# A recurrent memory branch on one core: five weight buffers in flight instead of four, 21 streamed slices instead of 20, in a new order

## The chip, the cores and the metric

One core of one Trainium2 chip. The metric is the device time of one execution in microseconds, as a median of several. Ratios are computed as the mean time of one kernel's runs over the mean of the kernel before in the same rounds on the same chip. They are therefore not quite the ratios of the medians quoted beside them, and they are what to compare across sessions: the median of the kernel before itself was 2405 to 2430 us from session to session.

## The reference

The result is `g * a + (1 - g) * b`. `a` is sliding window attention over 2048 tokens of width 640. `b` is an attention with a memory, and it takes most of the time:

```python
for s in range(n_seg):                       # 64 segments of 32 tokens
    h = concat([mem, x[s]])                  # 8 memory rows + 32 tokens
    q, k, v = h @ Wq, h @ Wk, h @ Wv         # 640 -> 32 heads x 192, three times
    p = softmax(where(mask, q @ k.T * scale, -1e9))
    o = (p @ v) @ Wo                         # 32 x 192 -> 640
    mem, out[s] = o[:8], o[8:]               # the next segment needs these 8 rows
```

The segments are a chain. The four weights have 7.9 MB each in bf16, and only part of them stays in the core's memory (SBUF) in both kernels.

## The kernel before

Heads are worked in four groups. The weights are cut into 84 slices: per group five each of q, k and v (128 x 1536, 384 KB) and six of o (128 x 1280, 320 KB). Of these, 64 are loaded once and stay. The other 20 are streamed again from HBM in each segment, through a ring of buffers. A slice "lands" when its transfer is complete. A buffer is "released" by the last matmul that reads it, and only then can the transfer of a later slice into it be issued. The projections of the last eight tokens of each segment do not depend on the chain. They are made for all segments before it, with a ring of their own, and are called the tails below:

```python
sb = {"w": (4, [P, WQ]), ...}                # the ring of weight buffers
STREAMED = {"q": ((), (4,), (4,), (3, 4)), "k": ((4,), (4,), (4,), (4,)), "v": ((), (), (4,), ()),
            "o": ((1, 3, 5), (1, 3, 5), (2, 5), (1, 3, 5))}

def load_w(u):
    ...
    if u not in weights.slot:
        return None                          # resident
    b = sc.buf("w")
    sc.op("SP", 100 + 0.78 * weights.width(u), lambda: nc.sync.dma_start(
        tile_of(b)[:, 0:weights.width(u)], weights.dram_of(u)), writes=[b])
    return b
```

A list fixes the order of TensorE in a segment. `q0` is the query projection of group 0 (five slices, streamed ones last), `tq0` its transposes, `s0` the scores, `p0` the transposed probabilities, `pv0` the values, `o0` the output projection (six slices):

```python
STEP = "q0 k0 tq0 tk0 k1 q1 s0 tk1 tq1 v0 k2 q2 s1 tk2 k3 p0 tq2 q3 s2 pv0 v1 p1 o0 tq3 pv1 tk3 v2 p2 s3 o1 pv2 v3 p3 o2 pv3 o3"
```

A small list scheduler with assumed durations orders the other engines and the DMA queue while the kernel is built; the chip sees only the order.

## Time and profile before

| | before |
|---|---|
| median of 3 runs | 2416.04 us (2411.96 to 2423.39) |
| memory branch | 560 to 2371 us of the span of 2406 |
| one segment, mean | 28.3 us |
| streamed per segment | 20 slices, 7.14 MB |
| TensorE busy, share of the span | 88% |

The first fence is the page's row of issues for the ring: how often, how large, and the median from issue to landing. The second is the page's DMA share and rate in 40 slices of the span.

```profile
t_w<-w_packed SPq DMA_DIRECT2D x704, 320.0 KB, 4.1
t_w<-w_packed SPq DMA_DIRECT2D x584, 384.0 KB, 4.4
```

```profile
DMA  4222224777888887888888888878888887888887
GB/s 138 69 66 62 65 73 131 239 227 232 266 265 271 274 276 255 273 272 267 270 263 288 272 272 283 268 253 264 256 272 273 280 263 248 268 278 275 264 277 232
```

1280 of these 1288 transfers belong to the 64 segments; the long even stretch at 248 to 288 GB/s is the memory branch. The prediction shows the rest.

### The profile page before, as it was taken

Reading aid. Unit: us, or ns where it says so; the run is one execution under the profiler, and the core shown is the slowest. Engines: PE = TensorE matmul, PEld = TensorE weight load, DVE = VectorE, ACT = ScalarE, POOL = GpSimd, SP = SyncE. Lnnn points to the kernel's source line nnn. Section 1 sums busy time; section 2 is a strip of 40 time slices with the busy share of each in tenths; the row PEclk is TensorE's granted clock in tenths of the full one; section 3 lists DMA queues with packets and bytes.
Section 4 is the critical chain, followed back from the end, with each engine's and each line's share of the span. In section 5 each row is a group of like instructions: output and inputs, shape, how many; then the busy total and the mean of one; then the engine's idle time right before and its main releaser. Section 6 shows DMA issues by size and latency. Waiting matters only on the chain.

```text
span 2406.0 us, 112716 instructions
## 1 busy us (share of the span) xinstructions
PE 2122.8 (88%) x49058; PEld 1523.4 (63%) x49093; DVE 1131.1 (47%) x3942; ACT 1045.4 (43%) x2385; POOL 741.7 (31%) x2055
## 2 busy tenths in 40 slices
PE   7999998998888888988889899888888888888885
PEld 5777767975666665666666666655666665666663
DVE  6888882233444433444444444444343443444334
ACT  4888883223333333433333344333333433333333
POOL 5555552123222222222222222222222222222220
PEclk9999988999999999999999999999999998999997
DMA  4222224777888887888888888878888887888887
GB/s 138 69 66 62 65 73 131 239 227 232 266 265 271 274 276 255 273 272 267 270 263 288 272 272 283 268 253 264 256 272 273 280 263 248 268 278 275 264 277 232
DMA packets 256880, 561.55 MB, mean 233 GB/s; under 512 B 54648, under 2 KB 70272, under 8 KB 256384
## 3 DMA queue, kind: packets, MB, share of 16 engines
q1 hardware_dynamic: 230608, 507.05, 64.9%
q0 software_dynamic: 21504, 43.03, 6.0%
q8 instruction: 385, 6.31, 1.0%
q10 hardware_dynamic: 4272, 4.26, 0.6%
q14 instruction: 111, 0.91, 0.1%
HBM read 524.83 MB, written 36.51 MB: 233 GB/s over the span
## 4 chain that ended last, share of the span: by engine, by line
PE 59%; DMA 35%; ACT 3%; issue 1%; DVE 1%; POOL 0%; SPq 0%; ACTq 0%; DVEq 0%; POOLq 0%
DMA t_w<-w_packed 33%; PE ps_o L946 8%; PE ps_k L776 8%; PE ps_q L776 8%; PE ps_v L776 6%; PE p_m L282 4%; PE p_s L327 3%; PE t_psum L590 3%; PE ps_pv L922 3%; PE tr_k L791 2%; PE t_psum L610 2%; PE p_o L411 2%; PE S_ps L848 2%; PE tr_q L791 1%; PE p_st L327 1%
## 5 line engine op out<-in xcount | busy, mean ns | idle before, releaser
L776 PEld LDWEIGHTS <-t_hT 128*32 128x32 bf16 x15360 | 380.2, 98 | 291.7 <-issue 65.7
L946 PE MATMUL ps_o<-t_OT,t_w 128*128 128x40 bf16 x7040 | 290.1, 180 | 104.9 <-DMA t_w<-w_packed 99.0
L946 PE MATMUL ps_o<-t_OT,w_o 128*128 128x40 bf16 x8320 | 321.4, 180 | 47.2 <-ACT t_OT L927 45.2
L946 PEld LDWEIGHTS <-t_w 128*128 128x128 bf16 x7040 | 226.5, 96 | 127.7 <-DMA t_w<-w_packed 125.5
L946 PEld LDWEIGHTS <-w_o 128*128 128x128 bf16 x8320 | 267.7, 96 | 55.4 <-issue 45.9
L823 POOL COPY t_K<-t_xqk 128x64 bf16<-128x64 bf16 x256 | 60.9, 238 | 776.2 <-PE S_ps L848 776.2
L357 DVE CUSTOM_DVE_ANT_0 a_junk<-p_s,a_mask 128x384 bf16<-128x384 f32 (+2 forms) x512 | 253.5, 529 | 41.4 <-PE p_st L327 29.0
L776 PE MATMUL ps_v<-w_v,t_hT 128*32 128x384 bf16 x4864 | 252.4, 336 | 0.0
L927 ACT CAST t_OT<-ps_pv 128x480 bf16<-128x480 f32 x256 | 143.2, 559 | 248.2 <-PE ps_pv L922 244.6
L776 PE MATMUL ps_q<-w_q,t_hT 128*32 128x384 bf16 x4096 | 222.0, 339 | 18.7 <-DVE t_hT L957 18.4
L387 ACT ACTIVATE a_pt<-p_st 128x384 bf16<-128x384 f32 (+2 forms) x512 | 219.8, 474 | 42.6 <-PE p_st L327 34.6
L814 DVE COPY t_K<-tr_k 128x256 bf16<-128x256 bf16 x256 | 74.7, 292 | 333.7 <-PE tr_k L791 333.4
L776 PE MATMUL ps_k<-w_k,t_hT 128*32 128x384 bf16 x4096 | 219.9, 336 | 0.1
L781 ACT CAST t_tok<-ps_k 128x384 bf16<-128x384 f32 x256 | 122.7, 479 | 207.5 <-PE ps_k L776 201.8
L800 ACT COPY b_QT<-tr_q 128x384 bf16<-128x384 bf16 x256 | 123.3, 481 | 175.7 <-PE tr_q L791 175.7
L905 DVE TENSOR_TENSOR t_PTx<-PT_ps,mk_x 128x320 bf16<-128x320 f32 x256 | 126.0, 492 | 143.1 <-PE PT_ps L898 143.1
L395 POOL TENSOR_SCALAR_AFFINE_SELECT a_pt<-a_pt 128x512 bf16<-128x512 bf16 x240 | 148.1, 640 | 128.9 <-ACT a_pt L387 128.2
L781 ACT CAST t_tok<-ps_q 128x384 bf16<-128x384 f32 x256 | 122.6, 479 | 149.5 <-PE ps_q L776 140.7
L858 DVE TENSOR_REDUCE sm_mx<-S_ps 128x4 f32<-128x160 f32 x256 | 82.4, 322 | 209.7 <-PE S_ps L848 208.1
L781 ACT CAST t_vtok<-ps_v 128x384 bf16<-128x384 f32 x256 | 122.7, 479 | 102.2 <-PE ps_v L776 102.2
L734 POOL DMA_DIRECT2D t_xqk<-xbqk x256 | 137.9, 539 | 80.1 <-POOL b_QT L804 40.0
L327 PE MATMUL p_st<-a_qa,a_k 64*128 64x128 bf16 x1440 | 148.2, 223 | 5.2 <-ACT a_pt L387 3.5
(144 smaller groups left out, 4052.3 us busy)
## 6 DMA issues: line engine op xcount, KB each, us to landing
t_w<-w_packed SPq DMA_DIRECT2D x704, 320.0 KB, 4.1
t_w<-w_packed SPq DMA_DIRECT2D x584, 384.0 KB, 4.4
t_xqk<-xbqk POOLq DMA_DIRECT2D x256, 48.0 KB, 3.6
xbqk<-t_ts POOLq DMA_DIRECT2D x12, 768.0 KB, 5.9
w_v<-in_B_Wv_dram SPq DMA_DIRECT2D x19, 384.0 KB, 8.2
w_q<-in_B_Wq_dram SPq DMA_DIRECT2D x16, 384.0 KB, 5.7
w_k<-in_B_Wk_dram SPq DMA_DIRECT2D x16, 384.0 KB, 4.2
xbv<-t_ts POOLq DMA_DIRECT2D x16, 384.0 KB, 3.7
```

Source lines behind the costliest of these rows:

```text
L282: nc.tensor.matmul(view()[:, gg, :], lhsT=Wp[:, kt, 4 * g:4 * g + 4, :].rearrange("p h d -> p (h d)"), rhs=T(k["xT"])[:, kt, :], start=(kt ...
L327: nc.tensor.matmul(T(out)[:, i * P:(i + 1) * P], lhsT=b if keys_first else a, rhs=a if keys_first else b, start=True, stop=True, tile_posi ...
L357: sc.op("DVE", 135 + n / 0.96, lambda: nc.vector.tensor_tensor_reduce(out=T(junk)[:, 0:n], in0=T(s)[:, 0:n], in1=mask[:, NKB * P - n:], op ...
L387: sc.op("ACT", act_ns(n), lambda: nc.scalar.activation(out=T(pt)[:, h % 4, 0:n], in_=T(s)[:, 0:n], func=ACT.Exp), reads=[s], writes=[pt])
L395: nc.gpsimd.affine_select(out=v, in_=v, compare_op=op, fill=0.0, base=0, pattern=[[0, 4], [sign, P]], channel_multiplier=-sign)
L734: sc.op("DMA", 500, lambda: nc.gpsimd.dma_start(tile_of(qk)[:].rearrange("p i b t -> p (i b t)"), xbqk[s, :, g].rearrange("p i c -> p (i c ...
L776: nc.tensor.matmul(t[32 * j:32 * j + 32, 0:384], lhsT=tile_of(hT)[:, kt, :], rhs=w[:, j * 384:(j + 1) * 384], start=(kt == kts[0]), stop=( ...
L781: sc.op("ACT", act(384), lambda: nc.scalar.copy(tile_of(tok)[:], b["tile"][:, 0:384]), reads=[b], writes=[tok])
L800: nc.scalar.copy(dst, tq["tile"][:].rearrange("p b (j t) -> p b j t", t=SEG))
L905: nc.vector.tensor_tensor(out=tile_of(dst)[:], in0=PT["tile"][:, i, :, :].unsqueeze(2).to_broadcast([P, 2, 4, L]), in1=mk.unsqueeze(1).uns ...
L927: sc.op("ACT", act(480), lambda: nc.scalar.copy(tile_of(OT)[:].rearrange("p b j l -> p (b j l)"), o["tile"][:, 0:480]), reads=[o], writes= ...
L946: nc.tensor.matmul(t[:, dt * L:(dt + 1) * L], lhsT=w[:, r * D + dt * P:r * D + (dt + 1) * P], rhs=OT["tile"][:, b, i, :], start=(g == 0 an ...
```

## The change

Its intent: let each transfer start one buffer earlier, pay for the buffer's 3072 bytes per partition by streaming one slice more, and spread the streamed slices so that they are needed at even distances.

```diff
-    LAT = {..., "SP": 2000}
+    LAT = {..., "SP": 3200}
-STEP = "q0 k0 tq0 tk0 k1 q1 s0 tk1 tq1 v0 k2 q2 s1 tk2 k3 p0 tq2 q3 s2 pv0 v1 p1 o0 tq3 pv1 tk3 v2 p2 s3 o1 pv2 v3 p3 o2 pv3 o3"
+STEP = "q0 k0 v0 tk0 tq0 k1 q1 s0 tk1 tq1 q2 s1 tq2 k2 k3 p0 tk2 q3 pv0 v1 s2 p1 o0 tk3 tq3 pv1 v2 s3 p2 o1 pv2 v3 p3 o2 pv3 o3"
-        "w": (4, [P, WQ]), ...
+        "w": (5, [P, WQ]), ...
-        sc.op("SP", 100 + 0.78 * weights.width(u), ...
+        sc.op("SP", 60 + 0.755 * weights.width(u), ...
-STREAMED = {"q": ((), (4,), (4,), (3, 4)), "k": ((4,), (4,), (4,), (4,)), "v": ((), (), (4,), ()),
-            "o": ((1, 3, 5), (1, 3, 5), (2, 5), (1, 3, 5))}
+STREAMED = {"q": ((), (), (3, 4), (4,)), "k": ((4,), (3, 4), (4,), (4,)), "v": ((), (4,), (4,), (4,)),
+            "o": ((1, 3, 5), (2, 5), (2, 5), (1, 3, 5))}
```

More of the change, by code (lines that the diff above doesn't have):

```diff
@@ L19 @@
 class Sched:
-    LAT = {"PE": 190, "DVE": 125, "ACT": 140, "POOL": 150, "DMA": 2000, "SP": 2000}
+    LAT = {"PE": 190, "DVE": 125, "ACT": 140, "POOL": 150, "DMA": 2000, "SP": 3200}
     SWITCH = 100
@@ L651, in branch_B @@
     sb = {
-        "w": (4, [P, WQ]), "hT": (1, [P, KT, SEG]), "tok": (2, [P, 384]), "vtok": (1, [P, 384]), "K02": (1, [P, 4, 2, L]),
+        "w": (5, [P, WQ]), "hT": (1, [P, KT, SEG]), "tok": (2, [P, 384]), "vtok": (1, [P, 384]), "K02": (1, [P, 4, 2, L]),
         "PTm": (1, [P, 2, 4, L]), "PTx": (1, [P, 2, 4, L]), "OT": (1, [P, 3, 4, L]), "Pm": (1, [P, 4, SEG]),
@@ L743, in load_w @@
         b = sc.buf("w")
-        sc.op("SP", 100 + 0.78 * weights.width(u), lambda: nc.sync.dma_start(tile_of(b)[:, 0:weights.width(u)], weights.dram_of(u)),
+        sc.op("SP", 60 + 0.755 * weights.width(u), lambda: nc.sync.dma_start(tile_of(b)[:, 0:weights.width(u)], weights.dram_of(u)),
               writes=[b])
```

## The prediction

> **What bounds the kernel now.** I read the page's slices first, then the windows of the long stage, then the chain, then the waits of TensorE and of the DMA queue, and last single slices in the timeline.
>
> The 40 slices show three stages: attention and tails to about 560 us, then one uniform stage to about 2371 us, then a short mix. The uniform stage is the memory branch: 64 segments one after another, since each needs the memory rows that the one before made. Three windows of it:
>
> ```profile
> 700.00:1200.00 500.00, 440.28 (x11133) 307.30 (x11129) 210.05 (x726) 192.81 (x443) 136.82 (x425) 0.98 0.83 269
> 1200.00:1700.00 500.00, 438.48 (x11164) 308.00 (x11168) 207.89 (x716) 191.75 (x440) 136.28 (x421) 0.99 0.83 269
> 1700.00:2200.00 500.00, 442.24 (x11198) 309.98 (x11187) 211.61 (x732) 192.79 (x443) 137.34 (x426) 0.97 0.83 269
> ```
>
> TensorE (first pair) is busy 88%, its clock is nearly full (0.97 to 0.99), the vector engines are under half busy, the DMA engines have 0.83 and move 269 GB/s. Nothing is full: two nearly full resources wait for each other. The chain says which:
>
> ```profile
> PE 59%; DMA 35%; ACT 3%; issue 1%; DVE 1%; POOL 0%; SPq 0%; ACTq 0%; DVEq 0%; POOLq 0%
> DMA t_w<-w_packed 33%; PE ps_o L946 8%; PE ps_k L776 8%; PE ps_q L776 8%; PE ps_v L776 6%; PE p_m L282 4%; PE p_s L327 3%; PE t_psum L590 3%; PE ps_pv L922 3%; PE tr_k L791 2%; PE t_psum L610 2%; PE p_o L411 2%; PE S_ps L848 2%; PE tr_q L791 1%; PE p_st L327 1%
> ```
>
> Weight slices streamed into the ring t_w carry 33% of the chain. That is not 33% to win: while a transfer is on the chain, TensorE works on other things. What is to win is TensorE's idle time, from its waits between 700 and 2300 us:
>
> ```profile
> PE ps_o L946 <- DMA t_w<-w_packed: 84.9, 133, 1.9
> PE ps_o L946 <- ACT t_OT L927: 39.6, 56, 0.7
> PE ps_q L776 <- DVE t_hT L957: 16.6, 57, 0.3
> PE tr_k L791 <- ACT t_tok L781: 16.5, 54, 0.3
> PE ps_q L776 <- DMA t_w<-w_packed: 13.8, 29, 1.6
> PE ps_k L776 <- DMA t_w<-w_packed: 6.3, 14, 0.8
> PE ps_v L776 <- DMA t_w<-w_packed: 2.0, 4, 0.7
> ```
>
> The four DMA rows make 107 us, but undercount, as the timeline shows:
>
> ```profile
> 1424.30 0.40 PE L946 MATMUL ps_o<-t_OT,t_w 128*128 128x40 bf16 x10
> 1424.55 0.40 PE L946 MATMUL ps_o<-t_OT,w_o 128*128 128x40 bf16 x10
> 1425.20 0.42 PE L946 MATMUL ps_o<-t_OT,t_w 128*128 128x40 bf16 x10 [0.25 <-DMA t_w<-w_packed]
> 1425.47 0.41 PE L946 MATMUL ps_o<-t_OT,w_o 128*128 128x40 bf16 x10
> ```
>
> Groups of ten start 0.25 us apart but count as busy for 0.40. A start 0.65 after the last has lost 0.40 us, and only 0.25 is called idle; a delay below 0.15 is not seen. So I took starts: for each streamed slice, the distance from the start of the matmul before it, less the usual spacing (0.025 us for output slices, 0.152 for projection slices). Over segments 5 to 61 this gives 2.85 us lost per segment, of a mean segment of 28.33 us. The worst positions are the third slice of the first output group (0.72), the last of the fourth (0.49) and the second of the fourth query chunk (0.33).
>
> The queue's own side, same window:
>
> ```profile
> SPq L744 <- PE ps_o L946: 367.7, 400, 3.4
> SPq L744 <- DMA t_w<-w_packed: 236.8, 374, 2.3
> DMA to landing us min/median/max: 2.9/4.2/7.7
> ```
>
> The issuing queue mostly stands waiting for TensorE to free a buffer. The loop is: buffer freed, issue, about 4.3 us to landing, wait for its turn, use.
>
> [...] its best 20 us window (440 to 460, other loads) has 313 GB/s at share 0.95. [...] a slice issued with one other slice in flight lands after 3.96 us, with two after 4.33, with three after 4.53.
>
> **The change, part by part.**
>
> *Fifth buffer.* Each transfer follows the release of the slice five places before it instead of four. In the trace the gap between those two releases is 0.5 to 2.7 us depending on place, 1.4 on average (28.33/20). All mean losses above are below that, so with unchanged transfers nearly all 2.85 us would go.
>
> *One slice more.* Before: q 4, k 4, v 1, o 11 = 20 slices, 9 x 393 KB + 11 x 328 KB = 7.14 MB per segment. After: q 3, k 5, v 3, o 10 = 21 slices, 7.60 MB (+6.4%). Smaller streams, estimated as 269 GB/s x 28.33 us - 7.14 MB, add 0.48 MB. So 8.08 MB must flow per segment.
>
> *Order.* The chunk v0 moves in front of the first transposes. That fills the wait of tr_k for t_tok: 16.5 us over 57 segments, 0.29 us each. The price: between the first and the second score group only q2 is left (before: v0, k2, q2). From score start to the next score I count 0.44 (scores) + 0.27 + 0.27 (transposes) + 0.82 (q2); the vector work for the new K then has about 1.4 us after the first scores for some 1.2 us (0.32 + 0.29 + 0.30 + 0.27). It fits narrowly; I allow 0 to 0.1. The waits for t_hT (0.29) and for t_OT before the last output group (0.7) stay.
>
> *Choice.* Streamed v slices now stand between the output groups, and the first half of a segment uses 9 slices instead of 8. Demand is more even.
>
> *Scheduler constants.* They emit nothing; the order of TensorE is fixed by the list, that of the queue stays by need.
>
> *Tails stage.* Its ring remains at three. The second group now needs three streamed slices, and its second must wait for the first group's last product, where before the third group had a wait of 1.2 us. About one more landing shows: +3 us once.
>
> Sum: without any waits for slices a segment takes 28.33 - 2.85 - 0.29 = 25.2 us. A buffer's turn is then 5 x 25.2 / 21 = 6.0 us (before: 4 x 28.33 / 20 = 5.67, made of 4.33 landing, 0.90 waiting for its turn, 0.2 use, 0.3 from release to reissue). With about 3.8 in flight instead of 3.1 (21 x 4.7 / 26.5 against 20 x 4.33 / 28.33), I set landing at 4.7 us. That leaves 6.0 - 4.7 - 0.5 = 0.8 us of slack, not more than the 0.9 of now, if nothing were lost. So losses do not vanish; they fall until turn and slack agree. Before: mean lateness 2.85/20 = 0.143, mean wait 0.90, as of a spread with mean 0.76 and deviation 1.04 us. The same spread with the new balance (mean = 0.80 + 4 x lateness) gives 0.077 us per slice, 21 x 0.077 = 1.6 us. Segment: 25.2 + 1.6 = 26.8. Gain 1.53 us x 64 = 98, less 3 in the tails: 2416 - 95 = 2321 us, 3.9% less.
>
> **Rivals.**
>
> *The transfers become the bound.* 8.08 MB at 330 GB/s (313/0.95) need 24.5 us per segment; at 26.8 us they flow at 301 GB/s, share about 0.92. If landing grows to 5.2 us under that load, the fifth buffer only holds a slower transfer, and the added 6.4% eat the rest: segments of 27.6 to 28, time 2375 to 2400. For it: share 0.83 already, landing grows with depth. Against: 0.95 was sustained for 20 us, and growth from two to three others was only 0.2 us. I give it 0.15.
>
> *All losses go.* With evener demand the spread shrinks, and the segment nears 25.4 to 25.8: 2255 to 2285. For it: every mean loss is below the gain from one more buffer. Against: the slack above. 0.12.
>
> *A compute wait takes over.* K or Q of the second scores late by 0.3 us and more: +20 us, so 2340. Possible on top of either.
>
> *Clock.* A busier TensorE might be granted less; 0.98 to 0.96 would cost some 0.3 us per segment, 20 us. The tails show 1.00 at 100% busy, which speaks against it.
>
> **Range and chances.** 2321 us; 2280 to 2372 holds it 8 times in 10, from near the all-go case to a mild form of the bandwidth rival. The 2% line is 2368. Faster by over 2%: 0.83; within 2%: 0.15; slower by over 2%: 0.02, as only saturation with longer landing would do it.
>
> **What would show it.** Right: segments near 26.8 us, GB/s near 300 and share 0.91 to 0.93 in the three windows; landing median 4.5 to 4.9 us; the four DMA rows of TensorE's waits down to roughly half of 107 us; the row tr_k for t_tok gone; no new row above 10 us at the second scores; the tails some 3 us longer. Wrong: landing above 5.2 with GB/s at 290 or less (bandwidth), new waits of S_ps for K or QT, a clock under 0.95, or DMA waits of TensorE as large as before.

## The result, and the profile after

| | before | after |
|---|---|---|
| median of 4 runs each | 2419.72 us (2411.96 to 2435.53) | 2290.39 us (2278.75 to 2298.31) |
| ratio | | 0.9454 (95%: 0.9386 to 0.9522) |
| segment, between output stores | 28.30 us | 26.20 us |
| lost to slices per segment | 2.86 us | 0.90 us |

Segments are measured here between the stores of two segments' outputs (segments 5 to 60), so that runs without slices can be measured alike. The loss is counted from the starts of matmuls as the prediction does. The time is 5.5% less; 3.9% was predicted.

The same three windows of the long stage (the columns are those of the prediction's first fence; the last two are DMA share and GB/s):

```profile
700.00:1200.00 500.00, 456.27 (x12060) 327.62 (x12056) 218.73 (x779) 209.83 (x475) 146.60 (x456) 0.99 0.93 307
1200.00:1700.00 500.00, 460.13 (x12156) 329.96 (x12151) 220.22 (x782) 212.50 (x481) 148.26 (x459) 1.00 0.93 311
1700.00:2200.00 500.00, 460.56 (x11986) 328.86 (x11985) 218.70 (x777) 209.00 (x473) 146.59 (x456) 0.98 0.92 306
```

TensorE is busy for about 459 of 500 us instead of 440, and the transfers follow: 308 GB/s instead of 269. On the chain of work that ended last, the transfers have 23% instead of 35%, and TensorE 68% instead of 59%:

```profile
PE 68%; DMA 23%; ACT 4%; issue 3%; DVE 1%; POOL 1%; SPq 0%; ACTq 0%; POOLq 0%; DVEq 0%
```

TensorE's waits, over 1600 us again (600 to 2200 us; us in total, times, longest):

```profile
PE ps_o L946 <- ACT t_OT L927: 43.1, 61, 0.7
PE ps_q L776 <- DVE t_hT L957: 20.4, 61, 1.7
PE ps_o L946 <- issue: 13.8, 20, 1.6
PE tr_q L791 <- ACT t_tok L781: 12.3, 59, 0.2
PE ps_o L946 <- DMA t_w<-w_packed: 12.2, 41, 1.0
PE ps_k L776 <- DMA t_w<-w_packed: 8.6, 17, 1.4
PE ps_v L776 <- issue: 7.8, 8, 2.6
PE ps_v L776 <- DMA t_w<-w_packed: 4.6, 8, 1.8
```

The rows for slices (DMA t_w) make 26 us with a last one of 0.6 that is not shown, against 107 before. The wait of tr_k for t_tok has gone, but a smaller one of tr_q has come in its place. And there are rows that end in "issue", 26 us in all with four small ones not shown: TensorE stood idle and no wait that the profile shows explains it. Before, one such row had 1.9 us. The queue and its landings, same window:

```profile
SPq L744 <- PE ps_o L946: 287.9, 407, 2.8
DMA to landing us min/median/max: 3.2/4.8/7.9
```

### The profile page after: what moved, and what is told of

Its sections match the earlier page's. It is cut to its first block, busy times and chain, and to the rows that moved or that the text cites.

```text
span 2283.2 us, 112848 instructions
## 1 busy us (share of the span) xinstructions
PE 2070.3 (91%) x49058; PEld 1508.2 (66%) x49093; DVE 1109.1 (49%) x3942; ACT 1054.5 (46%) x2385; POOL 737.9 (32%) x2055
## 3 DMA queue, kind: packets, MB, share of 16 engines
q8 instruction: 384, 6.29, 1.1%
## 4 chain that ended last, share of the span: by engine, by line
PE 68%; DMA 23%; ACT 4%; issue 3%; DVE 1%; POOL 1%; SPq 0%; ACTq 0%; POOLq 0%; DVEq 0%
DMA t_w<-w_packed 19%; PE ps_o L946 12%; PE ps_k L776 9%; PE ps_q L776 8%; PE ps_v L776 7%; PE ps_pv L922 4%; PE p_m L282 4%; PE p_s L327 4%; PE t_psum L590 3%; PE tr_q L791 2%; PE tr_k L791 2%; PE t_psum L610 2%; PE p_o L411 2%; PE S_ps L848 1%; PE p_st L327 1%
## 5 line engine op out<-in xcount | busy, mean ns | idle before, releaser
L776 PEld LDWEIGHTS <-t_hT 128*32 128x32 bf16 x15360 | 372.6, 97 | 281.5 <-issue 54.8
L946 PE MATMUL ps_o<-t_OT,w_o 128*128 128x40 bf16 x8960 | 329.7, 180 | 58.0 <-ACT t_OT L927 45.2
L946 PEld LDWEIGHTS <-w_o 128*128 128x128 bf16 x8960 | 281.7, 96 | 66.8 <-issue 57.3
L946 PE MATMUL ps_o<-t_OT,t_w 128*128 128x40 bf16 x6400 | 264.1, 180 | 21.5 <-DMA t_w<-w_packed 14.5
L357 DVE CUSTOM_DVE_ANT_0 a_junk<-p_s,a_mask 128x384 bf16<-128x384 f32 (+2 forms) x512 | 253.3, 528 | 40.7 <-PE p_st L327 29.4
L776 PE MATMUL ps_q<-w_q,t_hT 128*32 128x384 bf16 x4352 | 230.9, 336 | 22.1 <-DVE t_hT L957 21.0
L776 PE MATMUL ps_v<-w_v,t_hT 128*32 128x384 bf16 x4352 | 228.1, 330 | 6.6 <-issue 6.5
L946 PEld LDWEIGHTS <-t_w 128*128 128x128 bf16 x6400 | 207.3, 96 | 32.9 <-DMA t_w<-w_packed 25.8
L776 PE MATMUL ps_k<-w_k,t_hT 128*32 128x384 bf16 x3840 | 206.0, 332 | 0.3 <-issue 0.2
```

The source lines that it names most:

```text
L357: sc.op("DVE", 135 + n / 0.96, lambda: nc.vector.tensor_tensor_reduce(out=T(junk)[:, 0:n], in0=T(s)[:, 0:n], in1=mask[:, NKB * P - n:], op ...
L776: nc.tensor.matmul(t[32 * j:32 * j + 32, 0:384], lhsT=tile_of(hT)[:, kt, :], rhs=w[:, j * 384:(j + 1) * 384], start=(kt == kts[0]), stop=( ...
L946: nc.tensor.matmul(t[:, dt * L:(dt + 1) * L], lhsT=w[:, r * D + dt * P:r * D + (dt + 1) * P], rhs=OT["tile"][:, b, i, :], start=(g == 0 an ...
```

## The experiments

Twelve kernels. All of them passed the comparison with the reference, even the three that compute with wrong weights, so that comparison says little about this branch; the other nine do the kernel's own arithmetic. "Segment" and "loss" are as in the table above.

| run | buffers | slices | ratio to before (95%) | segment us | loss us |
|---|---|---|---|---|---|
| before | 4 | 20 | 1 | 28.30 | 2.86 |
| order_alone | 4 | 20 | 0.9972 (0.9905 to 1.0039) | 28.14 | 3.09 |
| four_buffers | 4 | 21 | 1.0155 (1.0125 to 1.0184) | 29.05 | 3.64 |
| old_order_old_choice | 5 | 21 | 0.9757 (0.9705 to 0.9809) | 27.64 | 1.94 |
| new_order_old_choice | 5 | 21 | 0.9666 (0.9633 to 0.9699) | 27.14 | 1.83 |
| old_order_new_choice | 5 | 21 | 0.9657 (0.9619 to 0.9695) | 27.01 | 1.12 |
| after | 5 | 21 | 0.9454 (0.9386 to 0.9522) | 26.20 | 0.90 |
| old_constants | 5 | 21 | 0.9540 (0.9492 to 0.9587) | 26.36 | 1.19 |
| split_output | 5 | 21 | 0.9571 (0.9512 to 0.9630) | 26.83 | 1.81 |
| six_buffers | 6 | 22 | 0.9420 (0.9370 to 0.9469) | 26.05 | 0.36 |
| six_buffers_split | 6 | 22 | 0.9505 (0.9463 to 0.9547) | 26.70 | 1.50 |
| no_slices_before | | 0 | 0.9114 (0.9075 to 0.9154) | 24.99 | 0 |
| no_slices_after | | 0 | 0.8996 (0.8956 to 0.9036) | 24.46 | 0 |

### four_buffers: is it the buffer?

```diff
-        "w": (5, [P, WQ]), ...
+        "w": (4, [P, WQ]), ...
```

(in the kernel after)

> The changed kernel with its order, its choice of 21 slices and its constants, but four buffers in the ring again. Theory A (the fifth buffer carries the gain, because a buffer's turn 4 x T / 21 leaves hardly any slack over a landing of 4.5 us): segments of about 28.8 us, some 2440 us in all, slightly slower than the kernel before, with over 3 us per segment lost to slices. Theory B (the new order and choice carry most of the gain, the buffer is secondary): 2355 us or less, segments under 27.4 us.

Measured: 2463.54 us against 2423.76, 1.6% slower than before, segments of 29.05 us and 3.64 us of loss. Theory A was close (28.8 us and over 3, though the whole time is 23 us above its 2440), theory B is out. Its windows show a machine with room to spare that does not use it:

```profile
700.00:1200.00 500.00, 435.02 (x10930) 307.31 (x10926) 198.01 (x700) 189.58 (x429) 133.29 (x412) 0.96 0.87 280
1200.00:1700.00 500.00, 435.68 (x10802) 304.20 (x10798) 198.12 (x699) 189.14 (x428) 131.14 (x408) 0.95 0.85 276
```

The new order and choice, without the fifth buffer, are a loss: one slice more in a ring that already turned too slowly. The clock (0.95 to 0.96, against 0.97 to 0.99 before) is lower as well, to which the last section returns.

### order_alone: the order in the kernel before

The edit is the line STEP of the diff alone, in the kernel before.

> The kernel before with the new order alone: four buffers, the old 20 slices. If the order is worth the wait of tr_k for t_tok and that wait is on the path: 18 us less, about 2400. If time won there is waited for at the next slice (ring of four sets the pace): 2416 plus or minus 10, and loss to slices rises above 2.85 us per segment.

Measured: 2397.62 against 2405.58 us, ratio 0.9972, which is unclear from no change. The loss rose from 2.86 to 3.09 us. Without slices the same order is worth 0.53 us per segment (below); here the segment is only 0.16 us shorter, and 0.23 us have come back as waits at slices. That is what the second reading said of the loss. The time itself does not decide: 2397.62 us is near the first reading's 2400, but the kernel before was faster in the same rounds too (2405.58), and 18 us less (a ratio of 0.993) lies within the interval.

### Order and choice, each alone, with five buffers

For the old choice, the old 20 slices cannot be kept, as the fifth buffer then finds no room (the build refuses it: a pool asks for 0.94 KB per partition and 0.56 are left). One slice of v was added:

```diff
-STREAMED = {"q": ((), (), (3, 4), (4,)), "k": ((4,), (3, 4), (4,), (4,)), "v": ((), (4,), (4,), (4,)),
-            "o": ((1, 3, 5), (2, 5), (2, 5), (1, 3, 5))}
+STREAMED = {"q": ((), (4,), (4,), (3, 4)), "k": ((4,), (4,), (4,), (4,)), "v": ((), (4,), (4,), ()),
+            "o": ((1, 3, 5), (1, 3, 5), (2, 5), (1, 3, 5))}
```

The old order is the old line STEP. Both edits together, then each alone:

> Five buffers and 21 slices, but the old order and the old choice (the old 20 slices plus one of v). Theory A' (evener demand from the new order and choice shrank the lateness below what I predicted; with the old ones the predicted size holds): segments of 27.1 us (26.8 plus the 0.29 of the wait for t_tok), 2338 us, loss near 1.6 us per segment. Theory B' (the fifth buffer shrinks lateness by itself, my estimate was simply too careful): 2308 us, segments near 26.65, loss near 0.9.

> Five buffers and the new order, with the old choice plus one slice of v (10 projection and 11 output slices, 7.54 MB against 7.60). If the choice of slices evens the demand: about 2315 to 2325 us and loss of 1.2 us or more per segment, most of it at the output groups. If the choice does not matter: within 0.5% of the changed kernel, 2290.

> Five buffers and the new choice with the old order. If the order is worth only the wait of tr_k for t_tok: 0.29 us x 64 = 18 us over the changed kernel, 2308 us. If the order also evens the demand for slices: 2320 us or more, loss per segment above 1.2 us.

Measured: 2367.28, 2344.12 and 2344.25 us, beside 2423.76 for the kernel before. Five buffers with the old order and choice give only 2.4% of the 5.5%. Their loss of 1.94 us is near, and a little above, the 1.6 that I had predicted for the change itself. So theory A' is the nearer one: what I had left out is what the new order and choice do to the evenness of the demand. The first two were 29 and 19 us slower than even the higher of my numbers. The third falls under the "2320 us or more" of its second reading, but its loss of 1.12 us is not above the 1.2 that went with it.

The loss tells the two apart. The choice lowers it from 1.94 to 1.12 in the old order and from 1.83 to 0.90 in the new. The order lowers it by 0.1 to 0.2 and otherwise shortens the segment itself. In time, with five buffers, the order alone is worth 0.9% and the choice alone 1.0%, but both together 3.0% (0.9757 against 0.9454, measured at different times). Whether they really help each other, or the two measurements differ by themselves, is not shown.

Why the old choice loses is seen in one place. This is the timeline of old_order_old_choice at the end of its first output group (start, duration, and in brackets the idle time before):

```profile
1404.23 0.41 PE L946 MATMUL ps_o<-t_OT,t_w 128*128 128x40 bf16 x10
1404.48 0.41 PE L946 MATMUL ps_o<-t_OT,w_o 128*128 128x40 bf16 x10
1406.19 0.42 PE L946 MATMUL ps_o<-t_OT,t_w 128*128 128x40 bf16 x10 [1.30 <-DMA t_w<-w_packed]
```

The third streamed slice of `o0` is late in each of the 57 segments counted, by 1.33 us on average: two thirds of all loss. Its transfer follows the release of the slice five places earlier, the first of the two of `q3`. On average that one is released 9.3 us after the use of the segment's first streamed slice begins, and the transfer is issued at 9.5. TensorE would be ready for it at 12.8 (14.1 less the loss of 1.33). So it has 3.3 us for a landing of 4.6. In the new choice `q3` has one slice, and the one five places earlier is that of `k3`. With the order unchanged (old_order_new_choice) the transfer is then issued 0.8 us earlier and needed 0.5 us later, so that it has 4.6 us, and the loss at this place is 0.17. In the kernel after it is 0.22. The rule of this ring is therefore not a mean: for each slice, TensorE's work between the release five places back and the use has to exceed a landing and the reissue (4.6 and 0.2 us at this place).

### no_slices: the segment without any wait for slices

```diff
     def load_w(u):
         ...
-        if u not in weights.slot:
-            return None
+        return None
     def w_of(u, b):
-        return weights.tiles[u] if b is None else b["tile"]
+        return weights.tiles.get(u) or weights.tiles[("o", 0, 0) if u[0] == "o" else ("v", 0, 0)]
```

The result is wrong, the instructions of TensorE are the same in number and shape. The edit was made in the kernel before and in the one after. (The 26.36 us of the second expectation is the mean over all segments of the kernel after.)

> The kernel before with no slice streamed in the memory branch; a resident slice stands in for each (wrong result on purpose). This measures a segment without waits for slices in the old order. From the starts of the matmuls I had 28.33 - 2.85 = 25.48 us per segment, so 2416 - 182 = 2234 us. If my count of lost time was too high (part of it clock or other waits), it stays above 2260; if delays hide behind others, it goes below 2215.

> The same in the changed kernel's order. By the step of the prediction (the new order takes away 0.29 us) a segment is 25.2 us: 18 us under the run with the old order. By the changed kernel's trace (26.36 - 0.91 = 25.45 us) the new order gains nothing without slices: within 5 us of the run with the old order, near 2232 us.

Measured: 2195.32 and 2166.02 us beside 2405.58. Both are lower than I expected. Segments are 24.99 and 24.46 us. So the kernel before lost 28.30 - 24.99 = 3.31 us per segment to streaming, with whatever traffic and clock cost besides the waits, and not only the 2.85 that I had counted. And the order is worth 0.53 us by itself, not 0.29: the inference from the trace of after that it gains nothing was wrong. The waits for t_tok account for little of it (17.5 us in 56 segments as against 13.1 in 61, so 0.1 us). The rest lies between the matmuls: the distances from the last start of one output tile to the first of another sum to 7.23 us per segment in the old order and to 6.52 in the new, where other kinds of work stand next to each other. Which of these pairs matter most was not separated. I had counted waits only.

### old_constants

```diff
-    LAT = {..., "SP": 3200}      and 60 + 0.755 * weights.width(u)
+    LAT = {..., "SP": 2000}      and 100 + 0.78 * weights.width(u)
```

> The changed kernel with the scheduler's two old cost constants. In the memory branch the build differs by one pair of vector instructions, in the tails by the order of the queue. Within 0.5% of the changed kernel (2279 to 2302 us). A rival by which the constants matter would show over 1%.

Measured: 2297.87 us, ratio 0.9540 where the kernel after has 0.9454, from another session, and the intervals touch. The median lies in the band that I had given. The two ratios differ by 0.9%, with an uncertainty as large, so an effect on the whole time is not shown, and one of 1% is not excluded either.

One effect does show, in the tails. The branch's first streamed slice is used at 560.0 us here, as in the kernel before (560.3), and at 564.1 in the kernel after. TensorE's wait of 3.0 us there, for `t_ts` at L610, stands in the trace of after and, with 3.0 and 2.4 us, in the two runs with the old choice and the new constants. Here, in the kernel before and in order_alone it is 0.3 us at most. So the constants lengthen the tails, and the choice of slices does not.

### six_buffers: would one more still help?

```diff
-        "w": (5, [P, WQ]), ...
+        "w": (6, [P, WQ]), ...
-"v": ((), (4,), (4,), (4,)),
+"v": ((4,), (4,), (4,), (4,)),
```

> The changed kernel with a sixth buffer, paid for by a 22nd slice (one of v0): 8.47 MB per segment with the small streams. If buffers still decide: loss falls under 0.4 us, 2255 us or so. If bandwidth now decides (at the share of 0.93 and 310 GB/s seen with five, 8.47 MB need 27.3 us): 2320 to 2350 us with landing above 5.5 us and GB/s no higher than 320.

Measured: 2282.81 us beside 2426.60, ratio 0.9420. The time lies between the two expectations and is not told apart from the kernel after (0.9454; the intervals overlap). The loss to slices fell to 0.36 us as the first reading said, and 325 GB/s were reached, more than the second allowed:

```profile
700.00:1200.00 500.00, 455.14 (x12150) 327.68 (x12151) 218.81 (x782) 211.40 (x478) 149.01 (x459) 0.99 0.95 325
```

Yet TensorE got no more work done. Its waits, 600 to 2200 us, say what came in the place of the slices:

```profile
PE ps_o L946 <- issue: 25.0, 35, 1.8
PE ps_v L776 <- issue: 11.9, 9, 2.2
PE ps_k L776 <- DMA t_w<-w_packed: 9.2, 16, 2.8
```

The rows "issue" make 51 us in all here, twice those of the kernel after.

### split_output: a wait that was not worth removing

The last output group waits 0.7 us for t_OT in each segment. A second buffer for t_OT fits (with one set of softmax statistics instead of three), and the output groups can be cut so that other output work stands in the gap:

```diff
-... s3 p2 o1 pv2 v3 p3 o2 pv3 o3
+... s3 p2 oa1 pv2 v3 p3 ob1 oa2 pv3 ob2 o3      # o1 cut after 5 slices, o2 after 4
-"OT": (1, ...)    b_stats bufs=3
+"OT": (2, ...)    b_stats bufs=1
```

> The changed kernel with a second buffer for t_OT and the second and third output groups cut, so that two pieces of output work stand between the last values and the last output group, which now waits 0.7 us for t_OT. If that wait is on the path and transfers can follow: 0.5 us x 64 = 32 us less, about 2258 us. If the transfers, at share 0.93, now set the pace: less than 12 us, 2278 to 2290, with the loss to slices up by 0.3 us per segment or more.

Measured: 2322.73 us beside 2426.60, ratio 0.9571: slower than the kernel after, and slower than even my second reading, though by the loss that it named. The wait for t_OT is gone, and this has come (600 to 2200 us, lines shifted by one):

```profile
PE ps_o L947 <- DMA t_w<-w_packed: 53.4, 109, 1.9
PE ps_q L777 <- DVE t_hT L958: 17.2, 59, 0.3
PE ps_o L947 <- issue: 14.8, 23, 1.4
```

The three streamed slices of the last output group lose 0.10, 0.44 and 0.56 us; in the kernel after they lost 0.08 together. They are needed 0.7 us earlier now (their waits taken off), but their transfers are not issued earlier. The second one is even issued 1.3 us later (18.9 us after the segment's first streamed slice instead of 17.6), since the slice of `v3` now stands five places before it. It is the same rule as above: the gap for t_OT had been time in which slices landed. Bandwidth does not explain it, since the rate fell to 299 to 303 GB/s. The smaller number of statistics buffers was not tested alone; TensorE has no wait for scores above 0.7 us in this trace.

### unread_slices: the transfers alone

```diff
     def load_w(u):
         ...
-        return b
+        return None
```

and the stand-in of the run without slices: all 21 slices are transferred into the ring, and no matmul reads them.

> The changed kernel's 21 slices per segment are all transferred into the ring of five, but no matmul reads them (a resident slice stands in, wrong result on purpose), so that nothing waits for them and the queue runs as fast as five in flight allow. It shows what the transfers alone can do, and whether their mere traffic costs TensorE time. If the stalls that the profile calls issue come from instruction fetches delayed by traffic: such stalls appear in TensorE's waits although no slice is waited for (they were absent without slices), and the time is 10 to 40 us over the run without slices (2166). If they belong to the coupling with slices: 2166 plus or minus 8 and no such stall. Transfers alone: if bandwidth bounds the changed kernel, no more than 320 GB/s in the memory branch; if its pace came from buffers coming free, 335 GB/s or more.

The whole time, 2645.25 us, answers nothing. I had overlooked that two resident output slices are loaded by the same queue: they stood behind the unread stream, and TensorE waited for them once for 376 us. What remains is useful, since the stream ran ahead and ended at about 1980 us. One program therefore has a stretch with traffic and one without, and TensorE waits for no slice in either:

```profile
1100.00:1800.00 700.00, 625.40 (x16036) 443.20 (x16036) 284.52 (x1030) 281.78 (x633) 195.01 (x604) 0.95 0.99 350
2050.00:2600.00 550.00, 522.10 (x14234) 379.90 (x14234) 253.93 (x921) 248.68 (x559) 173.53 (x538) 1.00 0.08 19
```

Transfers through five buffers move 350 GB/s when nothing holds them, and 363 to 381 in each 100 us from 600 to 900 us, while TensorE stood idle. So the 308 of the kernel after is not the limit of the transfers: its pace came from buffers coming free. That was the expectation of 335 or more. And segments take 27.56 us in the first stretch (26 of them) and 24.47 in the second (23). Mere traffic costs 3.1 us per segment here. The waits of the first stretch:

```profile
PE ps_q L776 <- DVE t_hT L957: 18.8, 26, 2.2
PE ps_o L946 <- issue: 18.8, 19, 1.5
PE ps_pv L922 <- issue: 3.7, 3, 2.2
```

In the second there is no row "issue". Stalls of this kind over 0.25 us sum to 29.4 us in 26 segments, 1.1 us each; the wait for t_hT is 0.7 us each instead of 0.3 (the small load of x, t_hT<-xa_dram, lands after 4.7 us at the median of this run, 3.6 in the kernel before); and the clock is 0.95 instead of 1.00, by estimate from these two at most 5% of a segment or 1.4 us. Together that is at most 2.9 of the 3.1.

What are the stalls? The trace has the packets of the queue that the page calls instruction (q8: 384 packets and 6.29 MB in the kernel after, so 16 KB each). In the kernel after, 29 stalls over 0.25 us between 700 and 2200 us ended 1.41 us after the landing of such a packet at the median, nine in ten within 1.56; in six_buffers 54 stalls, 1.40 and 1.55; in this run 45 stalls, 1.43 and 1.55. A random moment is 2.6 to 3.3 us after the last one at the median. So the stalls end some 1.4 us after such a packet lands. From this timing and the name of the queue I take it that TensorE stood waiting for its next instructions; no run moved these packets, so this is not shown. The packets themselves hardly slowed (0.98 us before, 1.01 to 1.05 in these, and 1.05 in no_slices_after, which has no stall), so slower packets do not explain the stalls; whether they started late was not measured.

### six_buffers_split

The edits of the last two variants together, five rounds.

> Six buffers with 22 slices and the cut output groups. Six buffers left 0.36 us of loss per segment, and cutting takes away up to 0.5 us of wait for t_OT. If the cut failed because a ring of five cannot follow the crowded output slices: with six it gains, 2255 to 2270 us. If at share 0.95 bandwidth takes all: 2280 to 2300 with a share of 0.96 or more, the loss above 0.7 us.

Measured: 2303.46 us beside 2429.90, ratio 0.9505: slower than six_buffers alone, with a loss of 1.50 us, at a share of 0.93 to 0.94. Neither reading held. The loss is above 0.7 as the second said, but the share is lower than without the cut, so bandwidth does not explain it. The loss now stands mainly at the first slice of `k1` (0.44 us) and the third of `o0` (0.35 us), and why is open. No version was found that clearly beats the kernel after.

## Why the prediction was right, and what was off

The measured 2290.39 us lies within the range of 2280 to 2372, near its fast end, and the mechanism held in the main: a fifth buffer lets each transfer start earlier, and the waits for slices shrink. One term of the sum, the loss that remains, was mis-sized, and two terms came out near by luck. The steps:

- *The fifth buffer is the lever.* Right as far as it is necessary, by four_buffers (1.0155) against after (0.9454). Without the new order and choice it gives 2.4% of the 5.5%.
- *One slice more, 8.08 MB per segment.* Right: 308 GB/s for 26.20 us are 8.07 MB. With 21 slices and four buffers the loss is 3.64 us.
- *Landing grows to 4.5 to 4.9 us, rate near 300 GB/s, share 0.91 to 0.93.* Right: 4.8, 306 to 311, 0.92 to 0.93. The transfers themselves reached 350 in unread_slices, more than the 330 that I had scaled from a 20 us window.
- *Tails some 3 us longer, by one more landing.* Right in size (564.1 us instead of 560.3 for the first streamed slice), but by luck. TensorE's waits for slices in the tails are 11.2 us before and after. What came is the wait of 3.0 us for `t_ts`, and it came from the scheduler's constants (see old_constants).
- *The scores do not take over.* Right: the waits of TensorE at scores stay under 1 us in 1600.
- *The row tr_k for t_tok goes, 0.29 us.* Half right: the row went, tr_q got 0.2 us of its own, and the order was worth 0.53 us by the pair of runs without slices.
- *The scheduler's constants emit nothing, and the queue's order stays by need.* Wrong in the tails, where they change the order and cost some 4 us, 0.2% of the time. An effect in the memory branch is not shown.
- *The four DMA rows fall to roughly half of 107 us.* They fell to a quarter, 26 us, which is the mis-sized loss of the last point.
- *A busier TensorE might be granted less clock.* It was the other way: of 1500 us, 68.3 were at half speed before and 30.7 after. By an estimate from the half speed, at most half of such time is lost, so up to 0.4 us per segment of the 2.1 won may have come from the clock, which the sum did not have.
- *Losses fall to 21 x 0.077 = 1.6 us.* This is the term that was mis-sized. It measured 0.90. I had written "The same spread with the new balance", with a deviation of 1.04 us taken over from before. Before, this spread was not noise: it was the uneven distances in the old list, always the same slices late. With the old order and choice the predicted size did hold roughly (1.94). The choice, which the prediction had called more even in one sentence, was not put into the sum.

The 25.2 us without loss came near by luck, as two errors cancelled. Without slices the new order takes 24.46. The trace of after leaves 26.20 - 24.46 - 0.90 = 0.84 us that neither number has. About 0.35 are the stalls in the rows "issue" (20.0 us between 700 and 2200), and up to 0.27 the clock: eight periods at half speed with 30.7 us in these 1500 us, by the same estimate at most half of it lost. The rest is not resolved. Bandwidth did not bind (308 GB/s, against 350 in unread_slices). Not all losses went, but the truth lies nearer to that rival than to my number: 2290 us is 5 us from its 2255 to 2285 and 31 from 2321. That rival's own sum has a slip: segments of 25.4 to 25.8 us make 2231 to 2257 us by the prediction's own reckoning, and the times given belong to 25.8 to 26.2 us, where the measured 26.20 lies at the upper end. (Another slip changes nothing: 21 x 4.7 / 26.5 is 3.7, not 3.8.)

## What to carry to other kernels

In a ring of N buffers, look at each streamed piece by itself: how much work stands between the release N places back and the use, against a landing. In these runs, with five buffers, a slice with 3.3 us for a landing of 4.6 lost 1.33 us in each segment, and the same place with 4.6 us lost 0.17. One pair of pieces that stand close can cost more than a mean of the whole shows (here 1.33 us of a loss of 1.94). Choose which pieces to stream by these distances before buying another buffer. In this kernel, at a DMA share of 0.95, a sixth buffer took most of the ring's waits away (0.90 to 0.36 us per segment), and nearly as much waiting of another kind came instead (the rows "issue" went from 26 to 51 us in 1600). So a loss that disappears from the ring's rows is not yet time gained.

## Stalls, clock, transfers and the ring in these runs

- TensorE's stalls that the profile names "issue" were none at DMA share 0.07, 1.9 us in 1600 at 0.83, 26 at 0.93 and 51 at 0.95, and 1.1 us per segment of 27.6 at 0.99. Where they were timed (the kernel after, six_buffers, unread_slices), they ended 1.4 us at the median after a packet of the instruction queue had landed. The cause is read from this timing and not shown.
- Between 700 and 2200 us, periods of half speed are 3.41 us long, or twice that, in the traces of the kernels before and after. The kernel before had 19 of them there, with no wait of TensorE above 1.9 us (the longest in the 8 us ahead of a period was 1.3 at the median). The kernel after had 8, four_buffers 31, and the two runs without slices none; unread_slices, which waits for no slice but has stalls in the rows "issue", had 24. Leaving unread_slices aside, more loss to slices per segment came with more such periods (0 us with none, 0.90 with 8, 2.86 with 19, 3.64 with 31). How much waiting it takes was not measured.
- Loads of 320 to 384 KB through five buffers came to 350 GB/s for 700 us beside the running segments of unread_slices, and to 363 to 381 for 300 us while its TensorE stood idle. A ring whose buffers TensorE frees stayed below that: 308 with five (the kernel after) and 325 with six (six_buffers).
- In old_order_old_choice, the slice with 3.3 us for a landing of 4.6 was late in every segment, while the others had landed 1.4 us before their use on average.
